# First block's h products in plain float32 from unsplit operands; the parts of w_in made one block later

## The chip, the cores and the metric

The program runs on one core of one Trainium2 chip. The metric is device time in microseconds (us) for one execution, lower is better. The engines are PE (TensorE: matmuls and transposes through the array), ACT (ScalarE), DVE (VectorE), POOL (GpSimd) and SP, whose queue issues most of the DMAs.

## What is computed

Three stages follow each other; only the middle one is touched by the change. Cut to what matters:

```python
# 1. chunked attention with 8 memory keys: q, k, v (4, 8, 768, 64) -> x (3072 tokens, 512)
# 2. a two-layer block with a rational activation
h = x @ w_in                                   # (3072, 512) @ (512, 2048)
P = a[0] + a[1]*h + a[2]*h**2 + a[3]*h**3
Q = 1.0 + abs(b[0])*abs(h) + abs(b[1])*h**2
x = (P / (Q + 1e-6)) @ w_out                   # (2048, 512)
# 3. a soft mixture of 8 experts with 4 slots each over all tokens:
#    logits = x @ phi, softmax over tokens and over slots, two small layers per expert
```

The inputs w_in and w_out reach the core as 64-bit floats; the kernel narrows them to float32 itself.

## The kernel before

The tokens are cut into six blocks of 512 (NBLK = 6), the 2048 columns of h into eight steps of 256 (NSTEP = 8). A step `kk` (0 to 47) is one block and one piece of 256 columns. `run_step` walks through a list of short names for each step: `h0`, `h1` issue the products of h for the next step, `a1` and `a2` the ScalarE part of the activation, `d1` and `t` its VectorE part, `p0`, `p1` the transposes of the finished activation (`post`), `x1` to `x3` the softmax over slots, and `at` one slice of the attention for the next block.

**The products of h.** In this kernel h is made from operands split in two parts, high and low, in the four-byte type F32R: `split_w` makes `wh` (an ACT copy, L326) and `wl` (a DVE subtraction, L327) from each piece of w_in, and the end of `attention` makes `xh` (ACT, L248) and `xl` (DVE, L249) from x. `h_part` then multiplies wh by xh, wh by xl and wl by xh: three products for each of four pieces of the contraction and for each half of the columns, 24 matmuls of 128 x 128 by 128 x 512 in a step (L343).

**The first block is different.** In steps 0 to 7 the kernel also loads and converts the weights. One piece of w_in comes with each step, is narrowed from 64 to 32 bits by `f64_narrow` (two ACT passes, L300 and L302; two DVE passes, L301 and L304) and split. The same is done to a piece of w_out (`narrow_w_out`), which is then written to DRAM by POOL, turned by eight PE transposes (`wp_chunk`, L438, with ACT copies L439 out of PSUM) and multiplied by phi (`wp_sum`, L446). From step 8 on the parts of w_in lie ready in 16 buffers of the pool `win`.

**What sets the order.** Up to the first product of h the order on each engine is written out by hand (`pre`). From there the program's order and a scheduler decide; each engine then works strictly in its own order. h of the next step goes into one of two PSUM tiles, which is free again when DVE has done its last read of the h before (L581). Three more PSUM banks (`m`) serve attention, transposes and conversion.

Of the kernel before, what the change touches and what calls it, by code (L numbers as in the profile page):

```python
# [10 lines left out]
F32 = mybir.dt.float32  # L11
F32R = mybir.dt.float32r
AF = mybir.ActivationFunctionType
# [6 lines left out]
def float_of_bits(u):  # L20
# [4 lines left out]
    'loads': "q0 q1 v0 i0 v1 c0 o0 i1 o1 q2 v2".split(),  # L25
    'pre': "f10 A A f5 B B A A A A B B A A B B A A A A s B B B B A A f2 A B B A s A B B A f2 B s B B B c f4 n t n t t".split(),
    'pre2': "i2 w0 z0 o2 n1 i3".split(),
    'ord0': "at a1 w1 s2 h0 d1 at t o3 z1 i4 n2 at a2 h1 p0 at p1 at at".split(),
    'ord': "at a1 h0 d1 at t a2 x2 h1 p0 p1 x1 at x3 at at".split(),
    'ordz': "d0 a1 t d1 a2 p0 p1".split(),  # L30
    'ordl': "a1 h0 d1 t a2 x2 h1 p0 p1 x1 x3".split(),
}
# [12 lines left out]
def tile_chunk_attention__rational__soft_moe(  # L45
# [97 lines left out]
    xt = {}  # L143

    def new_xt(b):
        xt[b] = [p_xt("xt", [P, NC, BLK], F32R) for _ in range(2)]

    def attention(pair, tile4=None, after=None):
        tile4 = tile4 or (lambda shape: p_a4("a4", shape))
        after = pair + 1 if after is None else after  # L150
        t_first = 2 * pair
        b = (t_first * P) // BLK
        qt, kt = ahead.pop(("q", pair))
        if pair < 2:
            both = ps_h("h", [P, 2, 2, HP, WIN])
            sc = [both[:, par] for par in range(2)]
        else:
            sc = [bank([P, 2, HP, WIN]) for _ in range(2)]
        for n in range(2):
            for hp in range(HP):  # L160
                for c in range(4):
                    for par in range(2):
                        r = slice(D * par, D * par + D)
                        o = P * n + CH * c
                        PE.matmul(
                            sc[par][CH * c:CH * c + CH, n, hp, :],
                            lhsT=qt[r, hp, o:o + CH],
                            rhs=kt[r, hp, 4 * n + c, :],
                            start=True, stop=True)
            yield  # L170
        if after < NPAIR:
            load_qk(after)
        pr = tile4([P, 2, HP, 2, WIN])
        rsum = []
        for par in range(2):
            for n in range(2):
                s0 = ((t_first + n) % TPB) * P
                if s0 == 0:
                    DVE.memset(sc[par][0:CH, n, :, 0:LEFT], NEG)
                if s0 + P == S:  # L180
                    DVE.memset(sc[par][P - CH:P, n, :, CTX - RIGHT:CTX], NEG)
            mx = p_sm("mx", [P, 2, HP], bufs=2)
            DVE.tensor_reduce(mx, sc[par], AX.X, ALU.max)
            yield
            e = pr[:, :, :, par, :]
            DVE.tensor_tensor(e, sc[par], mx.unsqueeze(3).to_broadcast([P, 2, HP, WIN]), ALU.subtract)  # L186
            ACT.activation(e, e, AF.Exp, scale=SCALE)  # L187
            yield
        pt = tile4([P, 2, HP, P])

        def sums():
            for par in range(2):
                sm = p_sm("sm", [P, 2, HP], bufs=4)
                DVE.tensor_reduce(sm, pr[:, :, :, par, :], AX.X, ALU.add)
                DVE.tensor_scalar(sm, sm, 1e-9, None, ALU.add)
                DVE.reciprocal(sm, sm)
                rsum.append(sm)
                yield

        def turns():  # L200
            turned = []
            for n in range(2):
                turned.append(bank([P, HP, P]))
                for hp in range(HP):
                    PE.transpose(turned[n][:, hp, :], pr[:, n, hp].rearrange("p a j -> p (a j)"), ident)
                if n == 0:
                    yield
            for n in range(2):
                ACT.activation(pt[:, n], turned[n], AF.Copy)
            yield  # L210

        for part in (turns, sums) if pair < 2 else (sums, turns):
            yield from part()
        vt = ahead.pop(("v", pair))
        if pair < 2:
            both = ps_h("h", [P, 2, 2, HP, D])
            pv = [both[:, par] for par in range(2)]
        else:
            pv = [bank([P, 2, HP, D]) for _ in range(2)]
        for n in range(2):  # L220
            for hp in range(HP):
                for c in range(4):
                    for par in range(2):
                        r = slice(WIN * par, WIN * par + WIN)
                        PE.matmul(  # L225
                            pv[par][CH * c:CH * c + CH, n, hp, :],
                            lhsT=pt[r, n, hp, CH * c:CH * c + CH],
                            rhs=vt[n][r, c, hp, :],
                            start=True, stop=True)
            if n and after < NPAIR:  # L230
                load_v(after)
            yield
        x_tok = tile4([P, 2, HP, 2, D])
        for par in range(2):
            DVE.tensor_tensor(x_tok[:, :, :, par, :], pv[par],
                              rsum[par].unsqueeze(3).to_broadcast([P, 2, HP, D]), ALU.mult)
            yield

        xh, xl = xt[b]
        for n in range(2):  # L240
            o = (P // TT) * ((t_first + n) % TT)
            pb = bank([P, HP, P])
            for hp in range(HP):
                PE.transpose(pb[:, hp, :], x_tok[:, n, hp].rearrange("p a d -> p (a d)"), ident)  # L244
            yield
            src = pb.rearrange("p h (r t) -> p h t r", t=TT)
            th, tl = (x.rearrange("p h (t r) -> p h t r", t=TT)[:, :, :, o:o + P // TT] for x in (xh, xl))
            ACT.activation(th, src, AF.Copy)  # L248
            DVE.tensor_tensor(tl, src, th.bitcast(F32), ALU.subtract)  # L249
            yield  # L250

    def attention_block(b):
# [53 lines left out]

    stage_in, stage_out = {}, {}
    scratch = [p_win("win", [P, 1024]) for _ in range(3)]
    win = {}

    def load_w_in(i):
        t = p_g("g", [P, NC, 2 * P, 2], U32)
# [3 lines left out]
    def load_w_out(i):  # L316
        t = p_g("g", [P, 2, DM, 2], U32)
        SP.dma_start(out=t.rearrange("p c f w -> p c (f w)"), in_=w_out[i])
        stage_out[i] = t

    def split_w(i):
        wh, wl = win[i] = [p_win("win", [P, NC, 2 * P], F32R) for _ in range(2)]
        src = stage_in.pop(i)
        yield from f64_narrow(src[:, :, :, 1], src)
        f = src[:, :, :, 1].bitcast(F32)
        ACT.activation(wh, f, AF.Copy)  # L326
        DVE.tensor_tensor(wl, f, wh.bitcast(F32), ALU.subtract)  # L327

# [7 lines left out]

    def h_part(step, tile_, f2):
        b, i = divmod(step, NSTEP)
        (wh, wl), (xh, xl) = win[i], xt[b]
        n = 0  # L340
        for ww, xx in ((wh, xh), (wh, xl), (wl, xh)):
            for c in range(NC):
                PE.matmul(tile_[:, f2, :], lhsT=ww[:, c, f2 * P:f2 * P + P], rhs=xx[:, c, :],  # L343
                          start=(n == 0), stop=(n == 3 * NC - 1))
                n += 1

    gts = {}
# [84 lines left out]
    def wp_chunk(i):  # L432
        t = wo.pop(i)
        ws = wos[i] = p_S("S", [P, 2, NC, P])
        for j in range(2):
            pb = bank([P, NC, P])
            for c in range(NC):
                PE.transpose(pb[:, c, :], t[:, j, c * P:c * P + P], ident)  # L438
            ACT.activation(ws[:, j], pb, AF.Copy)  # L439

    def wp_sum(i):
        pb = bank([P, 2, NSLOT])
# [27 lines left out]
    def convert(what):  # L470
        kind, n = what[0], int(what[1])
        if n < NSTEP:
            for _ in {"s": split_w, "n": narrow_w_out, "w": wp_chunk, "z": wp_sum, "i": load_w_in, "o": load_w_out}[kind](n) or ():
                pass

    new_xt(0)
    for what in KN["loads"]:
        load(what)
    gens = {"A": attention(0, after=NPAIR), "B": attention(1, lambda shape: p_T("T", shape), after=NPAIR),
            "s": split_w(0), "n": narrow_w_out(0), "t": split_w(1), "c": constants()}  # L480
    for what in KN["pre"]:
        if what[0] == "f":
            busy(int(what[1:]))
# [65 lines left out]
    def run_step(kk, what):  # L549
# [32 lines left out]
        elif what == "a2" and live:  # L582
            s, t, _ = act.pop(kk)
            w = p_S("S", [P, 2, BLK])
            for o in parts(kk):
                ACT.activation(w[:, o], s[:, o], AF.Ln, scale=2.0 ** -LN_SHIFT)  # L586
                ACT.activation(w[:, o], w[:, o], AF.Exp, bias=ex_b, scale=-1.0)  # L587
            late[kk] = t, s, w
        elif what == "d0":
            refine(kk - 1)  # L590
        elif what == "t":
            if kk - 1 in late:
                t, q, w = late.pop(kk - 1)
                e = near.pop(kk - 1)
                with tc.issue_after(behind[kk]) if kk in behind else nullcontext():
                    for o in parts(kk - 1):
                        DVE.scalar_tensor_tensor(t[:, o], t[:, o], a0, w[:, o], ALU.add, ALU.mult)  # L597
                        DVE.scalar_tensor_tensor(t[:, o], e[:, o], 2.0, t[:, o], ALU.subtract, ALU.mult, reverse0=True)  # L598
                gt_tile[kk - 1] = t
        elif what[0] == "x":  # L600
            n = int(what[1])
            if kk >= NSTEP and pi_ == (1, 2, 2)[n - 1]:
# [206 lines left out]
```

## Time and profile before

| what | value |
|---|---|
| median of three runs | 598.5 us (595.8 to 598.79) |
| the profiled execution | 597.04 us, of which its span (first to last instruction) 595.3 us |
| PE busy | 547.3 us, 92% of the span |
| DVE busy | 450.7 us, 76% |
| ACT busy | 417.8 us, 70% |
| POOL busy | 124.7 us, 21% |
| DMA, mean over the span | 164 GB/s |
| granted TensorE clock, mean | 0.96 of full speed |

The shares are means over stages with different limits. The span falls into four stretches: the attention of the first two pairs up to about 31.6 us, block 0 with the conversion of the weights (31.6 to 145.6 us, from the first product of h to the end of the products of step 8), the five blocks without conversion (some 66 us each, to about 474 us), and the experts at the end.

### The profile page before, as it was taken

The numbers are of one execution on the slowest core, as the hardware profiler recorded it, in microseconds if no ns is written. First come the engines' busy times: TensorE is split into PE (matmuls) and PEld (weight loads), VectorE is DVE, ScalarE is ACT, GpSimd is POOL, SyncE is SP. The second block draws the span as 40 slices with busy tenths as digits, with TensorE's granted clock in tenths as the row PEclk, the third lists the DMA queues.
The fourth block names the chain that finished last, engine by engine and source line by source line (L and its number), as shares of the span: only waits on it lengthen the run. The fifth ranks groups of instructions, "written<-read, shape, count | busy, mean of one in ns | idle before, by whom it ended". The sixth has DMA issues, their size and how long they took to land.

```text
span 595.3 us, 13669 instructions
## 1 busy us (share of the span) xinstructions
PE 547.3 (92%) x5944; PEld 390.6 (66%) x5944; DVE 450.7 (76%) x561; ACT 417.8 (70%) x542; POOL 124.7 (21%) x65
## 2 busy tenths in 40 slices
PE   6799699889999999999999999999999999679991
PEld 5677576667767777677776677776778577235351
DVE  4778999976987988878889698896887868820132
ACT  1589989976876868778777778687787869520132
POOL 0001221211313133131331223131322234300000
PEclk9699799898999999999999999999999999888996
DMA  8898975420221213202132022210365324969949
GB/s 350 355 334 319 362 291 225 133 81 1 107 73 45 69 67 107 73 25 85 72 108 73 1 107 72 108 34 39 108 238 187 134 82 153 381 247 355 410 178 358
DMA packets 21371, 97.41 MB, mean 164 GB/s; under 512 B 2624, under 2 KB 2752, under 8 KB 16320
## 3 DMA queue, kind: packets, MB, share of 16 engines
q1 hardware_dynamic: 20160, 92.35, 41.7%
q0 software_dynamic: 1152, 4.19, 1.7%
q8 instruction: 46, 0.75, 0.5%
q14 instruction: 13, 0.11, 0.1%
HBM read 86.05 MB, written 10.49 MB: 162 GB/s over the span
## 4 chain that ended last, share of the span: by engine, by line
PE 63%; DVE 13%; ACT 13%; issue 5%; POOL 2%; DMA 1%; SPq 0%; ACTq 0%; DVEq 0%; POOLq 0%
PE h L343 30%; PE m L369 4%; PE m L420 4%; PE lg L362 3%; ACT S L567 3%; PE h L670 3%; ACT S L568 3%; PE m L225 3%; ACT g L370 2%; PE m L446 2%; DVE T L580 2%; PE lg L707 2%; DVE T L581 2%; POOL S L544 2%; PE m L244 2%
## 5 line engine op out<-in xcount | busy, mean ns | idle before, releaser
L343 PE MATMUL h<-xt,win 128*128 128x512 f32 x1152 | 294.3, 404 | 7.3 <-ACT win L326 5.3
L343 PEld LDWEIGHTS h<-xt,win 128*128 128x128 f32 x1152 | 212.2, 191 | 55.3 <-ACT win L326 6.7
L544 POOL TENSOR_TENSOR S<-S,S 128x1024 f32<-128x1024 f32 (+1 forms) x49 | 118.3, 2416 | 306.8 <-DVE S L569 288.7
L567 ACT ACTIVATE S<-h,ctab 128x1024 f32<-128x1024 f32 (+1 forms) x49 | 53.9, 1101 | 58.4 <-PE h L343 56.3
L569 DVE SCALAR_TENSOR_TENSOR S<-S,S 128x1024 f32<-128x1024 f32 (+1 forms) x49 | 58.8, 1200 | 45.8 <-ACT S L568 45.6
L580 DVE TENSOR_TENSOR T<-T,h 128x1024 f32<-128x1024 f32 (+1 forms) x49 | 58.4, 1192 | 6.7 <-ACT T L570 6.7
L597 DVE SCALAR_TENSOR_TENSOR T<-T,ctab,S 128x1024 f32<-128x1024 f32 (+1 forms) x49 | 63.4, 1295 | 0.0
L369 PEld LDWEIGHTS m<-ident,T 128*128 128x128 f32 x384 | 44.3, 144 | 27.7 <-issue 13.4
L598 DVE SCALAR_TENSOR_TENSOR T<-S,T 128x1024 f32<-128x1024 f32 (+1 forms) x49 | 59.8, 1221 | 3.2 <-POOL S L544 0.5
L581 DVE SCALAR_TENSOR_TENSOR T<-T,ctab,h 128x1024 f32<-128x1024 f32 (+1 forms) x49 | 61.3, 1251 | 0.7
L570 ACT ACTIVATE T<-h,ctab 128x1024 f32<-128x1024 f32 (+1 forms) x49 | 59.2, 1207 | 0.0
L587 ACT ACTIVATE S<-S,ctab 128x1024 f32<-128x1024 f32 (+1 forms) x49 | 55.9, 1141 | 0.8
L586 ACT ACTIVATE S<-S 128x1024 f32<-128x1024 f32 (+1 forms) x49 | 51.7, 1055 | 6.7 <-DVE S L569 5.0
L369 PE MATMUL m<-ident,T 128*128 128x128 f32 x384 | 54.1, 282 | 1.9 <-DVE a L186 1.2
L370 ACT ACTIVATE g<-m 128x512 f32<-128x512 f32 x96 | 53.5, 603 | 3.1 <-PE m L369 2.9
L568 ACT ACTIVATE S<-h,ctab 128x1024 f32<-128x1024 f32 (+1 forms) x49 | 54.2, 1105 | 0.6 <-DVE T L597 0.6
L362 PE MATMUL lg<-T,wp 128*32 128x512 f32 x192 | 38.9, 614 | 5.4 <-DVE T L598 5.3
L187 ACT ACTIVATE a<-a 128x512 f32<-128x512 f32 x22 | 13.8, 638 | 19.6 <-DVE a L186 19.6
L420 PE MATMUL m<-g,s 128*32 128x512 f32 x192 | 23.5, 634 | 0.4 <-ACT s L412 0.4
L334 POOL DMA_DIRECT2D wo<-win x8 | 4.7, 589 | 86.6 <-DVE win L304 67.1
L249 DVE TENSOR_TENSOR xt<-m,xt 128x512 fp32r<-128x512 f32 x24 | 16.3, 687 | 7.9 <-ACT xt L248 7.9
L248 ACT ACTIVATE xt<-m 128x512 fp32r<-128x512 f32 x24 | 14.3, 606 | 9.6 <-PE m L244 9.6
(167 smaller groups left out, 626.3 us busy)
## 6 DMA issues: line engine op xcount, KB each, us to landing
win<-in_moe_w_dram SPq DMA_DIRECT2D x32, 512.0 KB, 4.7
k<-in_kw_dram SPq DMA_DIRECT2D x11, 1024.0 KB, 6.6
v<-in_vw_dram SPq DMA_DIRECT2D x11, 1024.0 KB, 5.0
g<-in_moe_w_in_dram SPq DMA_DIRECT2D x8, 1024.0 KB, 6.6
g<-in_moe_w_out_dram SPq DMA_DIRECT2D x8, 1024.0 KB, 9.4
out_dram<-win SPq DMA_DIRECT2D x12, 512.0 KB, 5.0
q<-in_qw_dram SPq DMA_DIRECT2D x11, 512.0 KB, 3.7
wo<-win POOLq DMA_DIRECT2D x8, 512.0 KB, 6.4
```

The costliest lines, as they stand in the source:

```text
L343: PE.matmul(tile_[:, f2, :], lhsT=ww[:, c, f2 * P:f2 * P + P], rhs=xx[:, c, :], start=(n == 0), stop=(n == 3 * NC - 1))
L369: PE.transpose(pb[:, m, f2 * P:f2 * P + P], t_[:, f2, tt * P:tt * P + P], ident)
L370: ACT.activation(gts[b, qd][:, 2 * part:2 * part + 2, 2 * P * o:2 * P * o + 2 * P], pb, AF.Copy)
L544: POOL.tensor_tensor(out[:, o], q[:, o], w[:, o], ALU.mult)
L567: ACT.activation(s[:, o], hh[:, o], AF.Abs, scale=b0)
L568: ACT.activation(y[:, o], hh[:, o], AF.Square, scale=rb1)
L569: DVE.scalar_tensor_tensor(s[:, o], y[:, o], QC, s[:, o], ALU.add, ALU.add)
L570: ACT.activation(t[:, o], hh[:, o], AF.Identity, bias=a2, scale=a3)
L580: DVE.tensor_tensor(t[:, o], t[:, o], hh[:, o], ALU.mult)
L581: behind[kk] = DVE.scalar_tensor_tensor(t[:, o], t[:, o], a1, hh[:, o], ALU.add, ALU.mult).ins
L597: DVE.scalar_tensor_tensor(t[:, o], t[:, o], a0, w[:, o], ALU.add, ALU.mult)
L598: DVE.scalar_tensor_tensor(t[:, o], e[:, o], 2.0, t[:, o], ALU.subtract, ALU.mult, reverse0=True)
```

## The change

In block 0 h is computed from unsplit operands in plain float32: x of that block is stored once, without `xl`, and a step has 8 matmuls in place of 24 (a plain float32 product shows as two records in the trace), and w_in is only narrowed, into a tile `w_f` of its own. The split into `wh` and `wl` happens six steps later (step 6 splits piece 0, step 13 piece 7), under the new name `y`, placed behind the last ACT pass of that step (`issue_after`). Besides, every second copy of a turned piece of w_out out of PSUM goes to DVE in place of ACT. For pieces 4 to 7 `w_f` lies in the four buffers `x`, which the end of the kernel fills with w_out rows.

```diff
-    'ord': "at a1 h0 d1 at t a2 x2 h1 p0 p1 x1 at x3 at at".split(),
+    'ord': "at a1 h0 d1 at t a2 y x2 h1 p0 p1 x1 at x3 at at".split(),
...
     def new_xt(b):
-        xt[b] = [p_xt("xt", [P, NC, BLK], F32R) for _ in range(2)]
+        xt[b] = [p_xt("xt", [P, NC, BLK], F32R if b else F32) for _ in range(2 if b else 1)]
...
-            th, tl = (x.rearrange("p h (t r) -> p h t r", t=TT)[:, :, :, o:o + P // TT] for x in (xh, xl))
-            ACT.activation(th, src, AF.Copy)
-            DVE.tensor_tensor(tl, src, th.bitcast(F32), ALU.subtract)
+            xs = [x.rearrange("p h (t r) -> p h t r", t=TT)[:, :, :, o:o + P // TT] for x in xt[b]]
+            ACT.activation(xs[0], src, AF.Copy)
+            if b:
+                DVE.tensor_tensor(xs[1], src, xs[0].bitcast(F32), ALU.subtract)
...
+    def narrow_w_in(i):
+        w_f[i] = (p_x("x", [P, 1024]) if i >= NSTEP // 2 else p_win("win", [P, 1024])).rearrange("p (c f) -> p c f", c=NC)
+        yield from f64_narrow(w_f[i].bitcast(U32), stage_in.pop(i))
+
     def split_w(i):
+        f = w_f.pop(i)
         wh, wl = win[i] = [p_win("win", [P, NC, 2 * P], F32R) for _ in range(2)]
-        src = stage_in.pop(i)
-        yield from f64_narrow(src[:, :, :, 1], src)
-        f = src[:, :, :, 1].bitcast(F32)
         ACT.activation(wh, f, AF.Copy)
         DVE.tensor_tensor(wl, f, wh.bitcast(F32), ALU.subtract)
...
     def h_part(step, tile_, f2):
         b, i = divmod(step, NSTEP)
-        (wh, wl), (xh, xl) = win[i], xt[b]
+        if b == 0:
+            pairs = [(w_f[i], xt[b][0])]
+        else:
+            (wh, wl), (xh, xl) = win[i], xt[b]
+            pairs = [(wh, xh), (wh, xl), (wl, xh)]
         n = 0
-        for ww, xx in ((wh, xh), (wh, xl), (wl, xh)):
+        for ww, xx in pairs:
             for c in range(NC):
                 PE.matmul(tile_[:, f2, :], lhsT=ww[:, c, f2 * P:f2 * P + P], rhs=xx[:, c, :],
-                          start=(n == 0), stop=(n == 3 * NC - 1))
+                          start=(n == 0), stop=(n == len(pairs) * NC - 1))
                 n += 1
...
-            ACT.activation(ws[:, j], pb, AF.Copy)
+            if j:
+                DVE.tensor_copy(ws[:, j], pb)
+            else:
+                ACT.activation(ws[:, j], pb, AF.Copy)
...
+        elif what == "y":
+            if 0 <= kk - 6 < NSTEP:
+                with tc.issue_after(st["exp"]):
+                    split_w(kk - 6)
```

Three places show what this does to the order of the engines. Behind the changed lines the line numbers shift: L343 becomes L349, L438 L444, L439 L446 (DVE) and L448 (ACT), L446 L455, L447 L456, L567 to L570 become L576 to L579, L580 and L581 L589 and L590, L597 and L598 L606 and L607, and L326 and L327 L328 and L329.

On PE, at the start of block 0, before the change (`h_587` is h of step 0; `m_615` and `m_621` are the turned pieces of w_out; `win_427`, `win_428` are wh and wl of piece 0):

```order
L343 MATMUL h_587<-xt_143,win_427 128x512 x4
L343 MATMUL h_587<-xt_144,win_427 128x512 x4
L343 MATMUL h_587<-xt_143,win_428 128x512 x4
L343 MATMUL h_587<-xt_143,win_427 128x512 x4
L343 MATMUL h_587<-xt_144,win_427 128x512 x4
L343 MATMUL h_587<-xt_143,win_428 128x512 x4
L438 MATMUL m_615<-ident_106,win_138 128x128 x4
L438 MATMUL m_621<-ident_106,win_138 128x128 x4
```

and after it (`h_576` is step 0, `h_680` step 1):

```order
L349 MATMUL h_576<-xt_143,win_426 128x512 x8
L444 MATMUL m_588<-ident_106,win_138 128x128 x4
L444 MATMUL m_594<-ident_106,win_138 128x128 x4
L349 MATMUL h_680<-xt_143,win_568 128x512
L455 MATMUL m_600<-u_110,S_587 128x32 x8
```

The 24 matmuls of step 0 have become 8, and the first one of step 1 has moved ahead of the product with phi, since its weight needs no split.

On ACT, at the same place, from the narrowing of w_in's piece 1 (`g_164`) to the activation of step 0, before the change:

```order
L302 ACTIVATE g_164<-g_164 128x1024
L439 ACTIVATE S_614<-m_615 128x512
L439 ACTIVATE S_614<-m_621 128x512
L326 ACTIVATE win_576<-g_164 128x1024
L447 ACTIVATE wp_109<-m_627 128x64
L567 ACTIVATE S_682<-h_587,ctab_108 128x1024
L568 ACTIVATE S_684<-h_587,ctab_108 128x1024
```

and after it (piece 1 is `g_163`):

```order
L302 ACTIVATE g_163<-g_163 128x1024
L448 ACTIVATE S_587<-m_588 128x512
L576 ACTIVATE S_655<-h_576,ctab_108 128x1024
L577 ACTIVATE S_657<-h_576,ctab_108 128x1024
L456 ACTIVATE wp_109<-m_600 128x64
```

One of the two copies and the split have left ACT's row, and the small copy of the product with phi stands behind the first two passes of the activation.

On DVE, in block 1, from step 8's activation to step 9's, before the change (`T` is the activation in work, `mx`, `a` and `sm` belong to the attention of the next block):

```order
L569 SCALAR_TENSOR_TENSOR S_1720<-S_1722,S_1720 128x1024
L580 TENSOR_TENSOR T_1721<-T_1721,h_1635 128x1024
L581 SCALAR_TENSOR_TENSOR T_1721<-T_1721,ctab_108,h_1635 128x1024
L597 SCALAR_TENSOR_TENSOR T_1629<-T_1629,ctab_108,S_1653 128x1024
L183 TENSOR_REDUCE mx_1810<-m_1686 128x8
L598 SCALAR_TENSOR_TENSOR T_1629<-S_1722,T_1629 128x1024
L186 TENSOR_TENSOR a_10_1809<-m_1686,mx_1810 128x8x64
L183 TENSOR_REDUCE mx_1814<-m_1687 128x8
```

and after it:

```order
L578 SCALAR_TENSOR_TENSOR S_1571<-S_1573,S_1571 128x1024
L589 TENSOR_TENSOR T_1572<-T_1572,h_1482 128x1024
L590 SCALAR_TENSOR_TENSOR T_1572<-T_1572,ctab_108,h_1482 128x1024
L606 SCALAR_TENSOR_TENSOR T_1476<-T_1476,ctab_108,S_1500 128x1024
L329 TENSOR_TENSOR win_1632<-win_675,win_1631 128x1024
L607 SCALAR_TENSOR_TENSOR T_1476<-S_1573,T_1476 128x1024
L183 TENSOR_REDUCE mx_1665<-m_1537 128x8
L183 TENSOR_REDUCE mx_1669<-m_1538 128x8
```

The subtraction of a split (L329) has come in between the last two passes of the step before, and the attention's first reduction has gone behind both. From block 2 on every engine's order is that of before.

## Rows read from the trace of the kernel before

**Rows 1.** Busy time of each engine by stretch; stretch, length, busy us (instructions), clock, DMA

```profile
31.60:145.60 114.00, 103.92 (x1014) 80.68 (x1016) 97.97 (x110) 100.08 (x125) 22.19 (x15) 0.93 0.60 221
60.00:75.00 15.00, 10.34 (x173) 8.11 (x172) 15.00 (x20) 14.44 (x17) 3.80 (x2) 0.77 0.92 364
145.60:211.00 65.40, 64.97 (x830) 47.38 (x830) 57.02 (x71) 51.40 (x66) 17.40 (x8) 1.00 0.23 82
```

**Rows 2.** Who waited for whom, 31 to 146 us: total us, times, longest

```profile
PE h L343 <- ACT win L326: 5.3, 3, 3.7
PE m L446 <- ACT S L439: 2.8, 3, 2.4
PE m L438 <- DVE win L304: 1.0, 1, 1.0
```

**Rows 3.** PE in order of time: start, length, line, what, count [idle before]

```profile
31.60 5.81 PE L343 MATMUL h<-xt,win 128*128 128x512 f32 x24 [1.05 <-ACT xt L248]
37.25 1.03 PE L438 MATMUL m<-ident,win 128*128 128x128 f32 x8
```

**Rows 4.** The line of a plain float32 product: min, median, max ns of its records

```profile
L380 PE MATMUL m<-s,stack x12: 591/592/697, 165.8 to 522.1; 128*128 128x512 f32 x12
```

**Rows 5.** The chain that ended last, around 166 us: start, us, what

```profile
165.97 0.86 PE m L380 x2
```

**Rows 6.** PE in order of time, equal groups in different stretches

```profile
53.91 2.10 PE L343 MATMUL h<-xt,win 128*128 128x512 f32 x8
...
68.54 2.64 PE L343 MATMUL h<-xt,win 128*128 128x512 f32 x8
...
110.75 4.56 PE L343 MATMUL h<-xt,win 128*128 128x512 f32 x12
...
118.13 0.98 PE L446 MATMUL m<-u,S 128*128 128x32 f32 x8
...
123.19 1.04 PE L369 MATMUL m<-ident,T 128*128 128x128 f32 x8
...
130.46 1.32 PE L446 MATMUL m<-u,S 128*128 128x32 f32 x8 [2.40 <-ACT S L439]
...
132.05 1.75 PE L446 MATMUL m<-u,S 128*128 128x32 f32 x8
133.62 1.52 PE L369 MATMUL m<-ident,T 128*128 128x128 f32 x6
134.79 10.85 PE L343 MATMUL h<-xt,win 128*128 128x512 f32 x40
...
148.49 3.02 PE L343 MATMUL h<-xt,win 128*128 128x512 f32 x12
```

**Rows 7.** Groups by line, 31.6 to 145.6 us and (L423) the whole span: busy, mean ns

```profile
L326 ACT ACTIVATE win<-g 128x1024 fp32r<-128x1024 f32 x7 | 8.0, 1143 | 0.4 <-DVE g L304 0.4
L327 DVE TENSOR_TENSOR win<-g,win 128x1024 fp32r<-128x1024 f32 x7 | 9.9, 1417 | 4.0 <-ACT win L326 4.0
...
L439 ACT ACTIVATE S<-m 128x512 f32<-128x512 f32 x16 | 9.3, 626 | 0.8 <-PE m L438 0.8
...
L423 DVE COPY u<-m x1: 682/682/682, 179.3 to 179.3; 128x512 f32<-128x512 f32 x1
```

**Rows 8.** Block 1, DVE, PE and ACT in order of time

```profile
162.76 1.27 DVE L581 SCALAR_TENSOR_TENSOR T<-T,ctab,h 128x1024 f32<-128x1024 f32 x1
164.08 1.89 PE L343 MATMUL h<-xt,win 128*128 128x512 f32 x7 [0.15 <-DVE T L581]
177.06 1.23 DVE L569 SCALAR_TENSOR_TENSOR S<-S,S 128x1024 f32<-128x1024 f32 x1 [1.41 <-ACT S L568]
195.31 0.63 ACT L187 ACTIVATE a<-a 128x512 f32<-128x512 f32 x1 [2.87 <-DVE a L186]
```

**Rows 9.** POOL and DVE in order of time, around 131 us

```profile
130.26 2.35 POOL L544 TENSOR_TENSOR S<-S,S 128x1024 f32<-128x1024 f32 x1 [3.44 <-DVE S L569]
...
131.13 2.57 DVE L327 TENSOR_TENSOR win<-g,win 128x1024 fp32r<-128x1024 f32 x1
```

More of the change, by code (lines that the diff above doesn't have):

```diff
@@ L27 @@
     'pre2': "i2 w0 z0 o2 n1 i3".split(),
-    'ord0': "at a1 w1 s2 h0 d1 at t o3 z1 i4 n2 at a2 h1 p0 at p1 at at".split(),
-    'ord': "at a1 h0 d1 at t a2 x2 h1 p0 p1 x1 at x3 at at".split(),
+    'ord0': "at a1 w1 s2 h0 d1 at t o3 z1 i4 n2 at a2 y h1 p0 at p1 at at".split(),
+    'ord': "at a1 h0 d1 at t a2 y x2 h1 p0 p1 x1 at x3 at at".split(),
     'ordz': "d0 a1 t d1 a2 p0 p1".split(),
@@ L237, in attention @@
             yield
-        xh, xl = xt[b]
         for n in range(2):
@@ L308, in tile_chunk_attention__rational__soft_moe @@
     scratch = [p_win("win", [P, 1024]) for _ in range(3)]
-    win = {}
+    win, w_f = {}, {}
     def load_w_in(i):
@@ L472, in convert @@
         if n < NSTEP:
-            for _ in {"s": split_w, "n": narrow_w_out, "w": wp_chunk, "z": wp_sum, "i": load_w_in, "o": load_w_out}[kind](n) or ():
+            for _ in {"s": narrow_w_in, "n": narrow_w_out, "w": wp_chunk, "z": wp_sum, "i": load_w_in, "o": load_w_out}[kind](n) or ():
                 pass
@@ L479, in tile_chunk_attention__rational__soft_moe @@
     gens = {"A": attention(0, after=NPAIR), "B": attention(1, lambda shape: p_T("T", shape), after=NPAIR),
-            "s": split_w(0), "n": narrow_w_out(0), "t": split_w(1), "c": constants()}
+            "s": narrow_w_in(0), "n": narrow_w_out(0), "t": narrow_w_in(1), "c": constants()}
     for what in KN["pre"]:
@@ L586, in run_step @@
                 ACT.activation(w[:, o], s[:, o], AF.Ln, scale=2.0 ** -LN_SHIFT)
-                ACT.activation(w[:, o], w[:, o], AF.Exp, bias=ex_b, scale=-1.0)
+                st["exp"] = ACT.activation(w[:, o], w[:, o], AF.Exp, bias=ex_b, scale=-1.0).ins
             late[kk] = t, s, w
```

## Prediction

> **What bounds the kernel now.** I read the page of the profile first, then the busy time by stretch, the waits of block 0, and PE in order of time. It says that PE is the fullest engine over the whole span, but the change acts on one stretch, and there three engines are equally full: from 31.6 to 145.6 us PE is busy 103.9 of 114 us, DVE 98.0 and ACT 100.1. In the block behind it, 145.6 to 211 us, PE is busy 65.0 of 65.4 us while DVE has 57.0 and ACT 51.4 [rows 1]. So from block 1 on PE alone sets the pace, and whatever lies on DVE or ACT is free as long as it is in time. In block 0 no engine is alone: PE loses 114 - 103.9 = 10.1 us waiting, and the waits say for what: 5.3 us for the ACT half of a split (L326), 2.8 us for the ACT copies of a turned piece of w_out, 1.0 us for a narrowing [rows 2].
>
> The waits cost PE more than their length. Around them the granted clock falls (mean 0.77 between 60 and 75 us [rows 1]; of the two levels, 2.4 and 1.2 GHz, the lower is then granted for part of the time), and equal groups take longer: eight products of h 2.64 us where others take 2.10, twelve 4.56 against 3.02, two groups of the phi product 1.32 and 1.75 against 0.98, six transposes 1.52 where eight take 1.04, and forty products 10.85 us [rows 6]. A full step of 24 takes 37.25 - 31.60 = 5.65 us, 0.235 each [rows 3], so forty should take 9.4 and a last drain of 5.81 - 5.65, 9.6. Together 0.54 + 1.54 + 1.11 + 0.48 + 1.25 = 4.9 us. So 15.0 of the 114 us are loss, 99.0 are PE's work at full clock.
>
> **What the change adds to PE.** The trace has plain float32 products of the new size, one to a block (L380). Each shows as two records of 592 ns [rows 4], which overlap: on the chain both together hold PE for 0.86 us [rows 5]. Eight of them are 6.9 us, against 5.65 us for the 24 before: 1.2 us more in a step, 9.8 us in the eight steps of block 0. Bounds: if the rate in a long row falls to 0.85, 9.2 us; if records don't overlap in a row, 16 x 0.592 = 9.5 us a step and 30.6 us in all. I take 9.8, since 0.86 was measured with a product of h ahead and others behind.
>
> **What it takes from ACT and DVE in block 0.** ACT loses seven splits (8.0 us) and eight of 16 copies of 0.63 us (5.0) and gets back two splits of 1.14 (pieces 0 and 1, in steps 6 and 7): 100.1 - 10.7 = 89.4 us. DVE loses the seven subtractions (9.9 us), gets eight copies out of PSUM at the 0.68 us of L423, and two subtractions of 1.22 (the seven less the one of 2.57, divided by six): 98.0 - 2.0 = 96.0 us [rows 7, 9]. The low halves of x that fall away are not counted. PE would have 99.0 + 9.8 = 108.8 us. So PE becomes the fullest engine here too, with the other two at about the shares of block 1.
>
> **Where the stalls go.** The added 9.8 us are bearable only if they fill waits. Most of them they should fill: the longest, 3.7 us for L326, stands ahead of step 3's products. The narrowing alone ends 1.14 us before the split did, and PE arrives later by the 1.2 us of each plain step since the start, some 2.5 us: nearly nothing is left, and I keep 0.3. Of the 2.8 us for copies I keep 1.2: two copies now run side by side, but one stands in DVE's full row. Of the rest I keep 0.5, and 1.0 us of low clock. Kept: 3.0 of 15.0. Block 0 then goes from 114 to 99.0 + 9.8 + 3.0 = 111.8 us, **-2.2 us**. Bounds: nothing kept, -5.2; all kept, +9.8. The start of the first product stays where it is: it waits for x's last ACT pass [rows 3], which doesn't move.
>
> **What block 1 pays.** Six splits lie there now, 1.14 us of ACT and 1.22 of DVE each. ACT goes to 58.3 of 65.4 us and has room. DVE goes from 57.0 to 64.3: 98%. Whether that is covered is read at single places [rows 8]. The products at 164.08 start when L581 (162.76 + 1.27) lets their PSUM tile go; a subtraction ahead of it in DVE's row comes straight through: 1.2 us. The next is absorbed by the 1.41 us in which DVE waits for ACT at 177.06. At 195.31 ACT waits 2.87 us for DVE, but only for the attention of the next block. I take one of the six uncovered, **+1.2 us**; the ends are 0 and 6 x 1.22 = 7.3 us. Behind block 1 the order of every engine is the old one; the loads of w_out rows into the `x` buffers move from block 0 to block 1, far ahead of their use, at no cost.
>
> **Sum.** -2.2 + 1.2 = -1.0 us, against the profiled execution's own 597.04 us (span 595.3): **596.0 us**. The median of the three runs is 1.5 us above that execution, their lowest 1.2 us below; I stay on the profiled one's scale and leave the difference to the range.
>
> **A rule that speaks against the change.** The row at 131.13 shows a subtraction of 2.57 us instead of 1.22: it began while POOL had its multiplication (130.26, 2.35 long), and ended about 1.1 us after that [rows 9]. The Trainium skill, SBUF — State Buffer, section "SBUF: two separate sides", says that a DVE pass with two SBUF inputs and a POOL pass that reads SBUF exclude each other for a whole instruction; by that rule every moved subtraction that meets POOL pays so. The row agrees.
>
> **Rivals.**
> 1. *All stalls go and block 1 covers the splits.* For it: PE is 99% busy in block 1 beside a DVE at 87%. Against: block 0's chains through narrowing, turning and phi are longer. 114 - 0.5 kept: -4.7 us, 592.3.
> 2. *DVE becomes the bound of block 1* (the other side). Place: the subtraction between the last two passes of each of steps 8 to 13. The price is 1.22 us for each that isn't covered, up to 7.3; from the third uncovered one on (2.2 / 1.22 = 1.8) the gain of block 0 is used up. For it: 98% load. Against: the idle time of 1.41 us, and PE's other work between two steps. With five uncovered: -2.2 + 6.1, 600.9.
> 3. *Block 0's stalls stay*, because DVE, hardly relieved, delivers narrowings and copies no sooner: only 5 of 15 us regained, +4.8 + 1.2, 603.0. For it: DVE still has 96 of 112 us, and narrowings stand in its row behind other work. Against: the waits name ACT more than DVE.
> 4. *Plain products don't overlap in a row*: 30.6 instead of 9.8 us, less 15.0 regained, +1.2: 613.8. The 0.86 us speak against it.
> 5. *The moved subtractions meet POOL.* 2.57 - 1.22 = 1.35 us for each of six, uncovered: 8.1 us more, 604.1. Against: between the pass that starts POOL (L569) and the subtraction stand three passes of some 1.2 us, and POOL needs 2.35.
>
> **How the numbers follow.** Forecast 0.42 (its own range 592.5 to 599.5), rival 1 0.21, rival 2 0.15, rival 3 0.14, rivals 4 and 5 0.04 each. About 0.5%, 3 us, is what a measurement of this kernel can tell from no change. Faster by more: rival 1 and two fifths of the forecast, 0.38. Slower by more: rivals 3 to 5 and a third of rival 2, 0.27. The same: 0.35. The range leaves out the upper part of rival 3 with 4 and 5, and the best of rival 1: 590.5 to 603.
>
> **What would show it.** In the profile after: groups of eight plain products (16 records) of about 6.9 us; the waits for L326 gone from block 0 and none of their size in their place; the granted clock near full between 60 and 146 us; the last product of step 8 near 143 us instead of 145.6; block 1 about 66.6 us instead of 65.4, with PE waits for L590. A step of plain products well over 7 us, or a PE wait for the DVE copies of the same size as the old ones, would make the forecast wrong; so would a block 1 of 70 us.

## The result, and the profile after

The changed kernel takes 590.63 us (median of 4 runs, 589.30 to 591.32) where the kernel before takes 597.38 us (median of 4, 595.80 to 598.79) on the same chip: ratio 0.9885, interval 0.9849 to 0.9921, so 1.15% faster, which is small but clear of the noise. The forecast was 596.0 us; the result lies inside its range of 590.5 to 603, at the very edge. The direction was right, the size was not: -1.0 us was worked out, -5.7 us came between the two profiled executions (597.04 and 591.32 us) and -6.7 us between the medians.

The busy time by stretch of the changed kernel: stretch, length, then busy us of PE, weight loads, DVE, ACT and POOL with their instructions, granted clock, DMA share, GB/s. They answer to [rows 1].

```profile
33.50:140.10 106.60, 103.66 (x949) 63.63 (x952) 94.61 (x110) 90.61 (x111) 22.18 (x15) 0.98 0.58 209
60.00:75.00 15.00, 13.63 (x191) 9.37 (x191) 15.00 (x16) 13.58 (x18) 4.35 (x3) 1.00 0.77 288
140.10:205.50 65.40, 64.95 (x831) 47.31 (x832) 62.02 (x76) 57.13 (x73) 16.30 (x8) 1.00 0.30 100
```

Block 0 went from 114.0 to 106.6 us. PE is now busy 103.66 of them; 2.9 us of idle time are left instead of 10.1, and the mean clock of the stretch is 0.98 where it was 0.93. The third row is a stretch of block 1 cut to the same 65.4 us as before; PE is as busy in it as before (64.95 us, 64.97 before), DVE 62.0 us in place of 57.0. Such a stretch is not a whole block, though the section on the kernel before gives the five blocks some 66 us each: it holds 163 records of products of h before, with 24 to a step, so about seven steps. From the first DVE pass of a block's activation (L569) to that of the next, the kernel before takes 75.1 to 76.3 us for blocks 1 to 4, and its last step begins this pass at 510.27 us. The experiments below measure whole blocks.

The waits of PE between 33 and 140 us in the changed kernel, as total us, times, longest; they answer to [rows 2].

```profile
PE m L455 <- DVE S L446: 1.9, 3, 0.8
PE m L225 <- ACT a L209: 0.5, 1, 0.5
PE m L444 <- DVE win L304: 0.3, 1, 0.3
PE m L444 <- ACT S L448: 0.3, 1, 0.3
```

No product of h waits for a split or for anything else any more. The largest wait is now for the copies of w_out that DVE makes (L446).

PE in order of time in the changed kernel, as start, length, line, what, count; the first two rows answer to [rows 3].

```profile
33.51 7.13 PE L349 MATMUL h<-xt,win 128*128 128x512 f32 x16
40.48 1.04 PE L444 MATMUL m<-ident,win 128*128 128x128 f32 x8
...
89.81 4.52 PE L349 MATMUL h<-xt,x 128*128 128x512 f32 x6
...
94.69 1.06 PE L368 MATMUL lg<-T,wp 128*32 128x512 f32 x8
...
121.68 1.06 PE L368 MATMUL lg<-T,wp 128*32 128x512 f32 x8
```

A step's eight plain products (16 records) hold PE for 40.48 - 33.51 = 6.97 us, 0.871 each, where 0.86 was forecast from one product.

**What the forecast did not look at** are the last two rows. A logits group is four matmuls that write four different groups of 32 PSUM partitions, two records each. The list scheduler decides what stands between them in PE's order, and the change moved that. These are the logits groups of the kernel before, PE in order of time:

```profile
78.03 1.04 PE L362 MATMUL lg<-T,wp 128*32 128x512 f32 x2
...
91.56 1.06 PE L362 MATMUL lg<-T,wp 128*32 128x512 f32 x6
...
100.31 1.05 PE L362 MATMUL lg<-T,wp 128*32 128x512 f32 x2
...
101.88 1.05 PE L362 MATMUL lg<-T,wp 128*32 128x512 f32 x2
...
121.18 1.05 PE L362 MATMUL lg<-T,wp 128*32 128x512 f32 x4
...
125.54 1.05 PE L362 MATMUL lg<-T,wp 128*32 128x512 f32 x4
```

One matmul alone takes 1.04 us, three 1.06 us, all four together 1.06 us: in these rows they run side by side only when they stand next to each other. The Trainium skill, TensorE: Matmul & The Clock Gate, section "Why this matters for your kernels", says that outputs at different groups of 32 partitions run as concurrent tiles; the rows agree, and add that a piece costs as much as the whole. In block 0 the line is busy 6.9 us before and 2.8 us after, by the rows below.

PE's groups of the changed kernel in block 0 by line (33.5 to 140.1 us): busy us, mean ns, idle before.

```profile
L349 PE MATMUL h<-xt,win 128*128 128x512 f32 x88 | 35.3, 541 | 0.0
L349 PE MATMUL h<-xt,x 128*128 128x512 f32 x64 | 33.0, 635 | 0.0
L455 PE MATMUL m<-u,S 128*128 128x32 f32 x128 | 15.7, 273 | 1.9 <-DVE S L446 1.9
...
L375 PE MATMUL m<-ident,T 128*128 128x128 f32 x40 | 5.6, 274 | 0.0
...
L368 PE MATMUL lg<-T,wp 128*32 128x512 f32 x20 | 2.8, 607 | 0.0
```

and three of the lines that stand for the same work before (31.6 to 145.6 us), which the change does not touch:

```profile
L446 PE MATMUL m<-u,S 128*128 128x32 f32 x128 | 17.2, 283 | 2.8 <-ACT S L439 2.8
...
L362 PE MATMUL lg<-T,wp 128*32 128x512 f32 x22 | 6.9, 606 | 0.0
L369 PE MATMUL m<-ident,T 128*128 128x128 f32 x40 | 6.7, 305 | 0.6 <-ACT a L209 0.6
```

The same 128 and 40 matmuls of L446 and L369 got 1.5 and 1.1 us cheaper. These sums count the overlap of a group with its neighbours; counted from each group's start to the start of the next, they got 0.9 and 0.8 us cheaper, at a mean clock of 0.98 instead of 0.93.

### The profile page after: what moved, and what is told of

It reads as the page before. It is cut to its first block, busy times and chain, and to the rows that moved or that the text cites. A ratio compares the mean times of both kernels' runs of the same rounds, so it can differ in the third digit from the quotient of the medians.

```text
span 589.5 us, 13536 instructions
## 1 busy us (share of the span) xinstructions
PE 547.0 (93%) x5880; PEld 376.9 (64%) x5880; DVE 451.8 (77%) x565; ACT 413.8 (70%) x534; POOL 124.3 (21%) x65
## 4 chain that ended last, share of the span: by engine, by line
PE 65%; DVE 15%; ACT 10%; issue 5%; POOL 2%; DMA 1%; SPq 0%; ACTq 0%; DVEq 0%; POOLq 0%
PE h L349 32%; PE m L375 4%; PE m L426 4%; PE lg L368 3%; ACT S L576 3%; PE h L683 3%; PE m L225 2%; ACT g L376 2%; ACT S L577 2%; PE lg L720 2%; DVE T L589 2%; DVE S L578 2%; PE m L455 2%; PE m L243 2%; DVE T L590 2%
## 5 line engine op out<-in xcount | busy, mean ns | idle before, releaser
L349 PE MATMUL h<-xt,win 128*128 128x512 f32 x1024 | 268.9, 411 | 0.7 <-DVE T L590 0.6
L349 PEld LDWEIGHTS h<-xt,win 128*128 128x128 f32 x1024 | 186.1, 188 | 48.5 <-issue 10.0
L576 ACT ACTIVATE S<-h,ctab 128x1024 f32<-128x1024 f32 (+1 forms) x49 | 53.8, 1099 | 55.2 <-PE h L349 53.8
L606 DVE SCALAR_TENSOR_TENSOR T<-T,ctab,S 128x1024 f32<-128x1024 f32 (+1 forms) x49 | 64.8, 1324 | 0.0
L589 DVE TENSOR_TENSOR T<-T,h 128x1024 f32<-128x1024 f32 (+1 forms) x49 | 58.3, 1190 | 7.2 <-ACT T L579 7.2
L590 DVE SCALAR_TENSOR_TENSOR T<-T,ctab,h 128x1024 f32<-128x1024 f32 (+1 forms) x49 | 61.3, 1251 | 0.8
L607 DVE SCALAR_TENSOR_TENSOR T<-S,T 128x1024 f32<-128x1024 f32 (+1 forms) x49 | 59.1, 1206 | 2.0
L579 ACT ACTIVATE T<-h,ctab 128x1024 f32<-128x1024 f32 (+1 forms) x49 | 59.2, 1208 | 0.0
L368 PE MATMUL lg<-T,wp 128*32 128x512 f32 x192 | 34.6, 612 | 4.9 <-DVE T L607 4.9
L349 PE MATMUL h<-xt,x 128*128 128x512 f32 x64 | 33.0, 635 | 0.0
L426 PE MATMUL m<-g,s 128*32 128x512 f32 x192 | 21.8, 595 | 0.4 <-ACT s L418 0.4
L302 ACT ACTIVATE g<-g 128x1024 f32<-128x1024 f32 x16 | 18.6, 1170 | 3.5 <-DVE g L301 3.5
```

The costliest lines, as they stand in the source:

```text
L576: ACT.activation(s[:, o], hh[:, o], AF.Abs, scale=b0)
L579: ACT.activation(t[:, o], hh[:, o], AF.Identity, bias=a2, scale=a3)
L589: DVE.tensor_tensor(t[:, o], t[:, o], hh[:, o], ALU.mult)
L590: behind[kk] = DVE.scalar_tensor_tensor(t[:, o], t[:, o], a1, hh[:, o], ALU.add, ALU.mult).ins
```

## The experiments

All times that follow are medians; the ratio is to the kernel before on the same chip, with its 95% interval. As a measure of block 0 that reads alike in every kernel, "block 0" below is the time from the start of the first product of h to DVE's first pass of the ninth step (31.60 to 149.36 = 117.76 us before, 33.51 to 144.37 = 110.86 us after); "block 1" is from there to the same pass eight steps later. Each block time is read from one execution: the changed kernel and after_group differ by 1.8 us in block 0 with the same order on PE there, so a difference below some 2 us says little by itself. The rows were measured on several chips, on which the kernel before takes 596.44 to 598.34 us, so they compare by their ratios.

| kernel | us | ratio | block 0 | block 1 |
|---|---|---|---|---|
| changed kernel | 590.63 | 0.9885 (0.9849 to 0.9921) | 110.86 | 75.78 |
| before_group | 602.52 | 1.0065 (1.0038 to 1.0093) | 117.85 | 77.94 |
| after_split_lg | 593.13 | 0.9923 (0.9893 to 0.9953) | 111.99 | 77.75 |
| after_nosub | 592.13 | 0.9895 (0.9861 to 0.9930) | 110.94 | 76.14 |
| after_group | 590.01 | 0.9857 (0.9823 to 0.9891) | 109.08 | 75.82 |
| before_tie | 595.65 | 0.9944 (0.9910 to 0.9977) | 116.57 | 75.51 |
| after_tie_actcopy | 589.86 | 0.9851 (0.9813 to 0.9890) | 108.29 | 75.78 |
| after_tie_early | 586.13 | 0.9797 (0.9757 to 0.9836) | 108.83 | 74.61 |
| before_tie_cut | 603.57 | 1.0103 (1.0070 to 1.0136) | 121.54 | 75.87 |
| before_tie_fill | 596.89 | 1.0003 (0.9973 to 1.0032) | 118.56 | 75.59 |
| after_tie_fill | 598.10 | 1.0006 (0.9974 to 1.0038) | 119.26 | 75.77 |
| after_tie_plain | 587.24 | 0.9841 (0.9803 to 0.9880) | 108.18 | 75.90 |

The kernel before has 75.89 us for block 1.

**before_group: whole logits groups in the kernel before.**

```diff
-                for j in range(4):
+                def logits(js):
+                    for j in js:
...
+                with tc.issue_after(logits((2, 3))):
+                    logits((0, 1))
```

> The kernel before, with one change: the four column-group matmuls of a logits product are tied together in TensorE's order, so that in block 0 the seven groups before its last product are no longer broken into pieces of one to three (34 pieces in the whole program become 29). Theory A (most of the gain that the forecast lacked came from TensorE's order, in which the changed kernel's logits groups stand whole, and not from the float32 products): block 0's first eight steps get 3 to 4 us shorter (a broken piece takes as long as a whole group, 1.04 to 1.06 us), and the run takes 593 to 594.5 us where before takes 597. Theory B (the pieces lie in time in which TensorE would wait for the split anyway): the waits for the split grow by what the pieces free, and the time stays within 1 us of before.

Block 0 takes 117.85 us against 117.76: theory A falls. The seven pieces of three groups became three whole groups, and nothing is gained. Theory B is right on block 0's time and wrong on where the freed time goes: the waits for the split are no longer (5.1 us, 5.3 before). PE is busy 106.84 us of block 0 instead of 107.69, at a mean clock of 0.90 instead of 0.93, so most of the time that the pieces freed seems to have gone into slower work. The run is even slower by 0.65%, outside theory B's 1 us: from block 1 on this tie breaks the groups as three and one at other places, block 1 takes 2.05 us more and the blocks behind it 1.7 more. PE is no busier in block 1 (75.57 us, 75.46 before), so the 2.05 us are idle time, of which the profile puts 1.3 us down to a wait for the first ACT pass of the softmax over slots (L383); why the new order brings it was not taken apart.

**after_split_lg: the logits of block 0 issued two and two, in the changed kernel.**

```diff
                 for j in range(4):
+                    if b == 0 and j >= 2:
+                        continue
...
+        if part and o and b == 0:
+            for j in (2, 3):
+                PE.matmul(st["lg"][32 * j:32 * j + 32, :], lhsT=wp[:, 4 * qd + j, :],
```

> The changed kernel, with the logits groups of block 0 issued as two and two, at the two halves of a step's transposes, so that they stand as pieces again. Theory A (whole groups are a large part of the gain): three of block 0's groups are broken inside its first eight steps, each for 1.04 us more, so block 0 ends 2 to 4 us later than in the changed kernel and the run takes 593 to 595 us. Theory B (TensorE has room in block 0 once the waits for the split are gone): the time stays within 1 us of the changed kernel's, 590.6 us.

The three broken groups cost 1.1 us in block 0 and 2.0 us in block 1 (two of the groups lie at block 0's end and behind it), 3.1 us in all, and 2.5 us of the median. PE's own busy time grows by nearly as much, 1.15 us in block 0 (107.92 to 109.07) and 1.97 us in block 1 (75.33 to 77.30), at the same mean clock. This is as theory A has it for the run (593 to 595 us), though the intervals of the two ratios overlap and block 0 alone stays below its 2 to 4 us. So the same pieces are free in the one kernel and paid in the other, as far as one execution of each shows, and the question becomes what sets the pace of block 0 in each.

**after_nosub: the subtraction of pieces 1 to 7 left out.**

```diff
+        wl = p_win("win", [P, NC, 2 * P], F32R) if i == 0 else wh
...
-        DVE.tensor_tensor(wl, f, wh.bitcast(F32), ALU.subtract)
+        if i == 0:
+            DVE.tensor_tensor(wl, f, wh.bitcast(F32), ALU.subtract)
```

> The changed kernel, without VectorE's subtraction for w_in's pieces 1 to 7: their low part is not computed, and the high part stands in for it. It measures what the moved splits cost block 1. The forecast's step: one of the six subtractions put into block 1 (1.2 us) lies on the path, so block 1 and the run get 1.2 us shorter, 589.4 us. Rival A (VectorE sets block 1's pace, all six are paid): 6 to 7 us shorter, 584 us. Rival B (TensorE sets the pace, which the 0.4 us between the two kernels' steps 8 and 16 speaks for): less than 0.5 us, 590.2 to 590.6 us.

Block 1 takes 76.14 us, not less than the 75.78 of the changed kernel, and the time is 592.13 us. The moved subtractions cost block 1 nothing: rival B, though the median lies above its range too. The rows of the changed kernel show why, DVE's subtractions between 140.1 and 205.5 us by form:

```profile
L329 DVE TENSOR_TENSOR win<-x,win 128x1024 fp32r<-128x1024 f32 x4 | 4.9, 1216 | 0.0
...
L329 DVE TENSOR_TENSOR win<-win,win 128x1024 fp32r<-128x1024 f32 x3 | 3.6, 1215 | 0.0
```

Seven of them, 8.5 us, none longer than the others (in the trace each begins after POOL's multiplication of that step has ended), on a DVE that is busy 62.0 of 65.4 us, while the only wait of PE in that stretch is 0.4 us for an attention pass. PE's own 64.95 us of 65.4 set the pace.

**after_group and before_tie: the same tie of the logits groups in both kernels.** Each group is issued behind the last transposes of the attention, in the same way in both; in blocks 1 to 4 all groups are then whole, in block 0 all of the changed kernel's and all but one of the kernel before.

```diff
-                PE.transpose(pb[:, hp, :], x_tok[:, n, hp].rearrange("p a d -> p (a d)"), ident)
+                st["att"] = PE.transpose(pb[:, hp, :], x_tok[:, n, hp].rearrange("p a d -> p (a d)"), ident)
...
+                with tc.issue_after(st["att"].ins):
```

> The changed kernel, with each logits group issued behind the attention's last transposes before it, which makes whole groups of the four that are still broken as one and three in blocks 1 to 4. Theory A (a broken group costs TensorE 1.05 us, and TensorE sets the pace of those blocks): 3 to 4 us less than the changed kernel, 586.5 to 587.6 us. Theory B (the pace of those blocks is set by VectorE or by the chain through the activation as much as by TensorE): less than 1 us, 589.6 to 590.6 us.

> The kernel before, with the logits groups issued behind the attention's last transposes before them, as in after_group: all but one of the groups in front of the tail stand whole (28 pieces instead of 34), one of block 0 is in three pieces. Against after_group it shows the change without the difference in TensorE's order of the logits. Theory A (in the kernel before, block 0 waits on the chain through the split, so that whole groups free nothing there; only blocks 2 to 4 get about 0.4 us each): 1 to 2 us below the kernel before, 596 us, and after_group is 6 to 7 us faster than this one. Theory B (TensorE's own work also sets block 0 of the kernel before): 3 to 5 us below it, 593 us, and after_group is only 3 us faster.

after_group takes 590.01 us. The median lies in theory B's range and 2.4 us above theory A's, but the intervals of the two ratios overlap. Behind block 1 its steps take 1.7 us less than the changed kernel's, half of what theory A expected and more than theory B. Its block 0 is 1.8 us shorter though PE's order there is the same: three products (six records) in the same place take 2.82 us where the changed kernel's row at 89.81 has 4.52, at a clock of 1.00 instead of 0.89 between 90 and 105 us. That stretch in the changed kernel, then in after_group, then PE in order of time in after_group:

```profile
90.00:105.00 15.00, 15.00 (x68) 8.38 (x68) 12.40 (x19) 11.22 (x15) 2.95 (x2) 0.89 0.48 189
```

```profile
90.00:105.00 15.00, 15.00 (x83) 9.47 (x82) 14.31 (x21) 13.23 (x19) 2.96 (x2) 1.00 0.55 205
```

```profile
86.20 1.97 PE L456 MATMUL m<-u,S 128*128 128x32 f32 x16 [0.72 <-DVE S L447]
88.01 2.82 PE L349 MATMUL h<-xt,x 128*128 128x512 f32 x6
```

before_tie takes 595.65 us, 2.3 us below the 597.98 of the kernel before on its chip, between theory A's 1 to 2 us and theory B's 3 to 5; block 0 is 116.57 us, 1.2 less. With the logits tied alike the change shortens block 0 by 116.57 - 109.08 = 7.5 us. The two medians differ by 5.6 us, just under theory A's 6 to 7 and well over theory B's 3, and the intervals of the ratios don't touch: the gain is the change's own, not the logits'.

**after_tie_actcopy, after_tie_early and after_tie_plain: the parts of the change.** The first puts both copies of w_out back on ACT; the second splits w_in two steps behind its own instead of six; the third does both, so that only the plain products, with x unsplit, remain.

```diff
-            if 0 <= kk - 6 < NSTEP:
+            if 0 <= kk - 2 < NSTEP:
...
-            if j:
-                DVE.tensor_copy(ws[:, j], pb)
-            else:
-                ACT.activation(ws[:, j], pb, AF.Copy)
+            ACT.activation(ws[:, j], pb, AF.Copy)
```

> after_group (the changed kernel with whole logits groups), with both copies of a turned piece of w_out on ScalarE again. Theory A (block 0 is set by TensorE's own work, and the copies only decide some 2 us of waits): within 1.5 us of after_group, 588.5 to 591.5 us. Theory B (the copies that ScalarE lost, 5.0 us, are what let its chain keep up): 3 to 5 us slower, 593 to 595 us.

> after_group, with w_in's piece split two steps behind its own step instead of six, so that six of the eight splits lie in block 0 again, as work that no product of block 0 waits for. Theory A (what paid is that the products of block 0 no longer wait for a split): block 0 ends within 1.5 us of after_group's, and the run takes 589 to 591 us. Theory B (what paid is the work that ScalarE and VectorE no longer have in block 0, 1.14 and 1.22 us for each split): four more splits there, 4.6 us of ScalarE and 4.9 us of VectorE, put block 0's end 4 to 5 us later, 594 to 595 us.

> after_tie_early, with both copies of a turned piece of w_out on ScalarE, as in the kernel before: of the change there remain the plain float32 products (with x kept unsplit) and a split that nothing in block 0 waits for, two steps later than before. Theory A (these alone are the gain): 585 to 588.5 us, as after_tie_early. Theory B (with the splits back in block 0, ScalarE can't do without handing the copies on): 3 to 5 us slower than after_tie_early, 589 to 591 us.

Theory A holds three times for block 0: 108.29, 108.83 and 108.18 us against after_group's 109.08, where theory B wanted 3 to 5 us more. Neither the copies handed to DVE nor the splits moved to block 1 pay for anything, and x's own split falls ahead of the first product, outside block 0 as measured here. With the splits in block 0 as work that nothing waits for, after_tie_early takes 586.13 us, 2.0% below the kernel before, and less than theory A's 589 to 591 us. Its interval doesn't touch the changed kernel's; it does overlap that of after_group, which differs from it by the place of the splits alone, so that the earlier place is better is likely and not shown. Its block 1 is 1.2 us shorter than after_group's; since after_nosub shows that the subtractions cost nothing there, what the 1.2 us are stays open. after_tie_plain's 587.24 us lie in theory A's range; its ratio overlaps both after_tie_early's and after_tie_actcopy's.

**before_tie_cut, before_tie_fill and after_tie_fill: PE's work taken away and added.** The first leaves out the product of w_in's low part in block 0 (16 products in a step instead of 24). The other two issue the first product of each half again, four times before and once after, and overwrite it.

```diff
-        for ww, xx in ((wh, xh), (wh, xl), (wl, xh)):
+        for ww, xx in ((wh, xh), (wh, xl), (wl, xh))[:3 if b else 2]:
```

```diff
-        n = 0
+        n = -4 if b == 0 else 0
...
-            for c in range(NC):
+            for c in (0,) * (4 * (n < 0)) + tuple(range(NC)):
...
-                          start=(n == 0), stop=(n == 3 * NC - 1))
+                          start=(n <= 0), stop=(n < 0 or n == 3 * NC - 1))
```

> before_tie, with 16 instead of 24 products in each of block 0's eight steps: low part of w_in times high part of x is left out there. It takes 8 x 8 x 0.235 = 15.1 us from TensorE's work. Theory A (the chain through ScalarE's split and VectorE sets block 0's pace in the kernel before): the eighth step gets at most 5 us earlier, and the waits grow by the rest. Theory B (TensorE's work sets it as much): 10 to 15 us earlier.

> before_tie, with 32 instead of 24 products in each of block 0's eight steps: the first product of each half is issued four times more, each time overwritten, so that the output stays that of the reference. It adds 8 x 8 x 0.235 = 15.1 us to TensorE's work. Theory A (block 0 of the kernel before waits on the chain through the split, and work of TensorE fills the waits and keeps its clock up): the eighth step ends at most 5 us later, 595 to 600 us. Theory B (TensorE's work sets block 0 of the kernel before): 10 to 15 us later, 606 to 611 us.

> after_group, with ten instead of eight plain float32 products in each of block 0's eight steps: the first product of each half is issued once more and overwritten, so that the output stays that of the reference. It adds 8 x 2 x 0.871 = 13.9 us to TensorE's work. Theory A (in the changed kernel TensorE's work sets block 0, since the products wait for no split): block 0 gets 10 to 14 us longer, 600 to 604 us. Theory B (the chain through ScalarE and VectorE still sets it, and there is room for more products): at most 5 us, 590 to 595 us.

In the kernel before, 15.1 us of products more make block 0 2.0 us longer, and 15.1 us less make it 5.0 us longer too, where theory A had expected "at most 5 us earlier" and theory B at least 10: both missed that one. In the changed kernel, 13.9 us more make it 10.2 us longer, within theory A's range, and the run 598.10 us, 2 us short of it. So in the kernel before block 0 is not set by the amount of PE's work, while in the changed kernel most of any added work is paid. What less work would do there was not run, and PE is not alone: of the 110.86 us the chain that ended last (the chain of work as the profile follows it back) still goes 39.6 us through DVE and ACT, narrowings above all, and three times it comes back to PE after a DVE copy that PE waited 0.55 to 0.75 us for. The busy time between 60 and 75 us shows what the work does, before_tie_cut first, then before_tie:

```profile
60.00:75.00 15.00, 11.38 (x163) 8.90 (x162) 14.90 (x17) 14.50 (x17) 3.68 (x2) 0.66 0.90 339
```

```profile
60.00:75.00 15.00, 9.96 (x171) 7.65 (x169) 15.00 (x20) 14.42 (x18) 3.52 (x2) 0.77 0.93 362
```

and before_tie_fill:

```profile
60.00:75.00 15.00, 14.41 (x208) 12.25 (x208) 15.00 (x16) 14.08 (x18) 4.21 (x3) 1.00 0.91 333
```

The clock goes 0.66, 0.77, 1.00 as the products go 16, 24, 32 to a step. Over the whole of block 0 the 15.1 us added to before_tie raise PE's busy time by 7.5 us only (107.09 to 114.63): 5.6 us of idle time are filled, the block is 2.0 us longer, and the other 7.6 us are mostly the same work done at a higher mean clock (0.97 instead of 0.91 in the same two stretches). Added work alone gains nothing, though: before_tie_fill's ratio is 1.0003. The waits of PE in before_tie (33 to 141 us):

```profile
PE h L343 <- ACT win L326: 5.1, 3, 3.7
PE m L447 <- ACT S L440: 1.6, 4, 0.8
```

The same stretch of before_tie_fill:

```profile
PE m L447 <- DVE a L235: 1.4, 1, 1.4
PE m L447 <- ACT S L440: 0.8, 2, 0.6
PE h L343 <- ACT win L326: 0.6, 1, 0.6
```

Of 5.1 us of waits for the split 0.6 are left: PE arrives later, and the added products lie where it would have waited. That PE's order changes with the number of products (the scheduler plans it anew) is part of these three results and wasn't separated from the clock.

## Why the prediction was right in direction and wrong in size

**What bounds the kernel** was read rightly: waits for the split and the clock around them in block 0, PE alone in block 1. The two fill runs show it for block 0, after_nosub and PE's 99% for block 1.

**The price of plain products**, 9.8 us, measured 8 x (6.97 - 5.65) = 10.6 us. They overlap in a row, so rival 4 is out.

**Where the stalls go** held in the main: PE's idle time fell from 10.1 to 2.9 us; the forecast kept 2.0 of waits, and 1.0 of low clock. The 1.2 us kept for copies are the 1.9 us for L446. But "two copies side by side" is worth nothing (after_tie_actcopy), and neither is the load taken from ACT and DVE (after_tie_early): what remains as the cause is that the products wait for the narrowing alone. Rival 3 is out.

**The step that failed** is the term "99.0 are PE's work at full clock", and with it "15.0 of the 114 us are loss". By it the changed kernel's PE would be busy 99.0 + 9.8 + 1.0 of low clock = 109.8 us in block 0; it is busy 103.66, 6.1 us less. By the lines: the logits have 6.9 - 2.8 = 4.1 us less, the price is 0.8 us more, and the rest, 6.1 - 4.1 + 0.8 = 2.8 us, is low clock that the forecast had counted as work. It had compared equal groups where it happened to find some, and taken 4.9 us, of which 1.0 was to stay. Counted from each group's start to the next, low clock gives back some 7 us: the products of h cost 57.9 us before and 64.2 after, 4.2 us less than the price of plain products adds, L446 and L369 give back 0.9 and 0.8, and small groups that the forecast had not compared another 1.0. The mean clock of [rows 1] would have said so: 0.07 x 114 = 8.0 us, an estimate from above, since the clock is also low while PE waits. Idle time is 0.9 us more than kept, so block 0 comes out 5.2 us below the forecast's 111.8. The 99.0 also took PE's order for fixed. In the kernel before, the broken groups were nearly free (0 us by before_group, 1.2 us by before_tie), so they were not loss either: they became a saving only because with the change PE's work in block 0 is mostly paid, and then the scheduler happened to set whole groups (after_split_lg, 3.1 us).

**Block 1** was forecast to pay 1.2 us; it pays -0.1 us, and nothing for the subtractions (after_nosub). Rivals 2 and 5 are out. The load of 98% for DVE put six subtractions, which belong to eight steps, into a stretch of seven; over the whole block DVE is busy 69.95 of 75.78 us, 92%. The seventh subtraction of the stretch from 140.1 us is that of step 7, at 141.69 us, ahead of the ninth step's first pass.

**The sum.** 596.0 - 5.2 - 1.3 = 589.5 us, against 591.32 measured. Between these lie differences that no edit touches: the first product of h starts 1.9 us later in this execution (33.51 instead of 31.60), the steps behind block 1 take 1.6 us more and the tail 2.3 us less. By these marks the spans (595.3 and 589.5 us) differ by 1.9 - 6.9 - 0.1 + 1.6 - 2.3 = -5.8 us, of which the change's own part, block 0 and block 1, is -7.0. What happened is rival 1 in all but its reason: its 592.3 us come from stalls that go altogether, while the run keeps 2.9 us of them and gains on PE's work.

## What to carry to other kernels

Before you add an engine's work up at full clock, take its granted clock over the whole stretch rather than a few equal groups, and look in the new order at every group whose parts run side by side, also where the change doesn't touch them. Where an engine waits for a chain, as PE did here, more work on it can be nearly free and less work can gain nothing; run one kernel with work added and one with work removed to know which case you have. If a product can use an operand one step earlier in its making, leave the later step where it is as work that nobody waits for: moving it out of the block bought nothing here.

## What the runs showed that was not expected

Taking 15.1 us of products out of a block made it 5.0 us longer, with the granted clock at 0.66 instead of 0.77 between 60 and 75 us. One of the four column-group matmuls costs 1.04 us, all four 1.06 us if nothing stands between them. Three plain products (six records), soon behind a wait of 0.75 us, took 4.52 us in one execution and, in another kernel with the same order around them, 2.82 us soon behind a wait of 0.72 us: 1.7 us that no edit made.
